# Scores of a batch's last two attention tasks in four quarters of the array, and another order of pools, in a fused attention and mixture-of-experts kernel

## The chip, the cores and the metric

One core of a Trainium2 chip runs one program. The metric is the device time of one execution in microseconds, as the median over runs. The kernel before takes 660.11 us (three runs, 658.83 to 661.78).

## What is computed

```python
def _attn_ref(q, k, v):                      # B, H, S, D = 8, 8, 576, 64
    scores = np.matmul(q, k.transpose(0, 1, 3, 2)) / np.sqrt(D)
    rel = pos[:, None] - pos[None, :]
    mask_local = (rel >= 0) & (rel < 32)
    mask_strided = (rel >= 0) & (pos[None, :] % 32 == pos[:, None] % 32)
    # heads 0 to 3 use mask_local, heads 4 to 7 mask_strided; softmax; times v

def _moe_ref(x, w_gate, w1, w2):             # N, D, E, F = 4608, 512, 8, 1024
    probs = softmax(x @ w_gate); expert = argmax(x @ w_gate)
    # row by row: probs[expert] * (relu(x @ w1[expert]) @ w2[expert])
```

The rows of x are the 4608 tokens with the outputs of their 8 heads side by side.

## The kernel before

**Attention.** Only the score blocks that a mask leaves are computed. The blocks of one batch are laid out in five tasks k = 0 to 4 (`BANK_PAIRS`), each of which fills one PSUM bank `s` of 128x512 f32. Tasks 0 and 1 are local heads, task 2 holds a rest of the local heads and three strided blocks, tasks 3 and 4 hold strided blocks alone, of 54x54 and, four in task 3, of 36x36. There are 40 tasks, and one loop goes over them in slots. In the slot of task i, the program emits in this order: the transposition of the probabilities of task i-3 (`stage_t`, L460, bank `t`), small steps from a queue (logits L535 and L542, rows of x L527, routing L577, L625), the scores of task i (`stage_s`), the load of q and k for task i+5 (`load_qk`, issued on SP), the product with v of task i-4 (`av_local` L485 or `av_strided` L474, banks `v`), and the load of v for a later task (`load_v`, SP). From batch 4 on, every slot also carries pieces of early expert windows (`filling`), which need expert weights (`raw`, L214, SP) that ACT casts to `whi` (L222) and DVE to `wlo` (L223).

TensorE runs in the order in which the program emits; the other engines and SP are ordered by a scheduler that estimates when each instruction can start. There are two banks `s`. Tasks take them in turn.

`stage_s` first adds the mask to the whole bank with one 128x512 matmul (L408), then adds the blocks. A strided block of the pair's head h reads partitions 64h to 64h+63 and writes the same partitions of the bank (L430): h = 0 uses one quarter of the array, h = 1 the quarter diagonally opposite. Then `softmax` follows on a bank: maximum `nm` (L357, DVE), subtraction into the tile `prob` (L360, DVE, the last reader of the bank), exponential (L361, ACT), sum `sm` (L363) and reciprocal `ri` (L365, L366, DVE), product `prob` (L367, POOL). ACT copies results out of PSUM (L162): `pT`, `xT`, `xr`.

**Experts.** `window` gathers 256 or 512 tokens of one expert by an indirect DMA on POOL (L240), splits them in two f32r parts, multiplies by w1 (L302 to L304, `t`), splits the result (`hh` L307 on ACT, `hl` L308 on DVE), multiplies by w2 (L291 to L293), scales (`finish`, L258 on ACT or L260 on DVE) and scatters the rows by an indirect DMA on POOL (L261). The main loop over `ORDER` starts with expert 1. Tiles of 32 tokens (`small`) have their weights loaded by ACT's queue (`sraw`, L1027, behind a register load from `srow`, L1005). The pools behind attention (`yp` for the output rows, `slp` for slots, `smp` for small tiles) are placed in SBUF that attention's pools have given back, in the order in which they are made. Who uses such a place first waits for its last user of before.

Of the kernel before, what the change touches and what calls it, by code (L numbers as in the profile page):

```python
# [1 line left out]

# [22 lines left out]
RG = 3 * SR  # L25
NRG = 11
LASTG = S - (NRG - 1) * RG
# [39 lines left out]
NBK = len(BANK_PAIRS)  # L67
WHERE = {p: (k, n) for k, ps_ in enumerate(BANK_PAIRS) for n, p in enumerate(ps_)}
LB = 16


def task_layout():
# [71 lines left out]
def moe_attn(ctx, tc, qk, vv, wg, wcat, blob0, blob, out):  # L144
    nc = tc.nc
# [7 lines left out]
    def bank(tag):  # L153
        return ps.tile([128, 512], F32, name=tag, bufs=BANKS[tag])
# [170 lines left out]
    with ExitStack() as actx:  # L325
# [76 lines left out]
            o = VV[k][0][key] + 128 * n  # L402
            return loaded[b, "v", k][:, o:o + 128]

        def stage_s(b, k):
            sb = bank("s")
            mk = 0 if k < 2 else k - 1 if k < 3 else 2
            nc.tensor.matmul(sb, identb, mask_b[:, mk].rearrange("p n k -> p (n k)"), start=True, stop=False)  # L408

            t = loaded.get((b, "qk", k))  # L410
            at = QK[k][0]

            def wide(m, i, last):
                j = 4 * m + i
                keys = qkl[k][:, LQ:].rearrange("p (h x) -> p h x", h=2)[:, :, QB * j:QB * j + 64]
                o = sb[QB * i:QB * i + QB, 256 * (m // 2):256 * (m // 2) + 256].rearrange("p (h y c) -> p h y c", h=2, y=2)
                nc.tensor.matmul(o[:, :, m % 2], qkl[k][:, QB * j:QB * j + QB], keys,  # L417
                                 start=False, stop=last, tile_position=(0, QB * i))

            def local(o0, nb, i, h, j, col, last):  # L420
                hs = slice(64 * h, 64 * h + 64)
                o = 64 * h + 32 * i
                q0 = o0 + QB * j
                k0 = q0 + QB * nb
                nc.tensor.matmul(sb[o:o + QB, col:col + 64], t[hs, q0:q0 + QB], t[hs, k0:k0 + 64],
                                 start=False, stop=last, tile_position=(64 * h, o))

            def strided(q0, k0, w, h, col, last):
                hs = slice(64 * h, 64 * h + 64)
                nc.tensor.matmul(sb[64 * h:64 * h + w, col:col + w], t[hs, q0:q0 + w], t[hs, k0:k0 + w],  # L430
                                 start=False, stop=last, tile_position=(64 * h, 64 * h))

            for n, (kind, hp, m) in enumerate(BANK_PAIRS[k]):
                if kind == "l":
                    for i in range(4):
                        wide(m, i, m == 3)
                    continue
                for y in range(2):
                    col = 128 * n + 64 * y
                    last = n == 3 and y == 1  # L440
                    if kind == "lx":
                        for i in range(2):
                            for h in range(2):
                                local(at["lx", i], 2, i, h, y, col, last)
                    else:
                        for h in range(2):
                            if kind == "s":
                                q0 = at["s", hp, m] + RG * y
                                strided(q0, q0 + 2 * RG, RG, h, col, last)
                            else:  # L450
                                q0 = at["sx", y]
                                strided(q0, q0 + LASTG, LASTG, h, col, last)
            return softmax(sb)

        pTs = {}

# [9 lines left out]
            evac("a", pT, tb)  # L466
            pTs[b, k] = pT

        def probs_of(b, pair, y, cols):
            k, n = WHERE[pair]  # L470
            return pTs[b, k][64 * y:64 * y + 64, 128 * n + cols.start:128 * n + cols.stop]

        def av_mm(av, c0, w, h, y, lhsT, rhs):
            nc.tensor.matmul(av[64 * h:64 * h + 64, c0:c0 + w], lhsT, rhs, start=True, stop=True, tile_position=(64 * y, 64 * h))  # L474
# [14 lines left out]
        def av_strided(b, hp, xT, off):  # L489
            av = [bank("v"), bank("v")]  # L490
            for t in range(5):
                vst = v_of(b, WHERE["s", hp, t][0], ("s", hp, t))
                for y in range(2):
                    for h in range(2):
                        av_mm(av[y], RG * t, RG, h, y, vst[64 * y:64 * y + RG, 64 * h:64 * h + 64],
                              probs_of(b, ("s", hp, t), y, slice(64 * h, 64 * h + RG))[0:RG])
            c1 = 5 * RG
            if hp == 0:
                for i in range(2):
                    vt = v_of(b, 2, ("lx", i))  # L500
                    for y in range(2):
                        for h in range(2):
                            av_mm(av[y], c1 + QB * i, QB, h, y, vt[64 * y:64 * y + 64, 64 * h:64 * h + 64],
                                  probs_of(b, ("lx", 0, 4), y, slice(64 * h + 32 * i, 64 * h + 32 * i + 32)))
            else:
                vst = v_of(b, 3, "sx")
                for y in range(2):
                    for h in range(2):
                        av_mm(av[y], c1, LASTG, h, y, vst[64 * y:64 * y + LASTG, 64 * h:64 * h + 64],
                              probs_of(b, ("sx", 0, 5), y, slice(64 * h, 64 * h + LASTG))[0:LASTG])  # L510
            xv = xT[:, 2 + hp, off:off + S].rearrange("p (a r) -> p r a", r=STR)
            for y in range(2):
                dst = xv[:, 0:30, :].rearrange("p (t y l) a -> p t y l a", y=2, l=3)[:, :, y, :, :]
                evac("a", dst, av[y][:, 0:c1].rearrange("p (t l a) -> p t l a", l=3, a=SR))
                if hp == 0:
                    x0 = off + 512 + QB * y
                    evac("a", xT[:, 0:2, x0:x0 + QB], av[y][:, c1:c1 + 2 * QB].rearrange("p (a q) -> p a q", q=QB))
                else:
                    xl = xT[:, 2 + y, off:off + S].rearrange("p (a r) -> p r a", r=STR)
                    evac("a", xl[:, 30:32, :], av[y][:, c1:c1 + LASTG].rearrange("p (r a) -> p r a", a=SR))  # L520
# [322 lines left out]
        tasks = [(b, k) for b in range(B) for k in range(NBK)]  # L843
# [25 lines left out]
        pvs = {}  # L869
        with tc.manual_schedule(engines={mybir.EngineType.PE}):  # L870
            for i in range(nt + LAG_AV):
# [4 lines left out]
                ia = i - LAG_AV  # L876
# [8 lines left out]
                    step()  # L885
                if i < nt:
                    filling()
                    pvs[i] = stage_s(*tasks[i])
                    load_qk(i + NBK)
                if 0 <= ia < nt:  # L890
                    if k == 0:
                        queue.extend(late)
                        late.clear()
# [43 lines left out]
    pools.append((wraw2, whl2))  # L937
    xgm = ctx.enter_context(tc.tile_pool(name="xgm", bufs=8))
    xtm = ctx.enter_context(tc.tile_pool(name="xtm", bufs=2))
    yp = ctx.enter_context(tc.tile_pool(name="yp", bufs=5))  # L940
    slp = ctx.enter_context(tc.tile_pool(name="slp", bufs=2))
    smp = ctx.enter_context(tc.tile_pool(name="smp", bufs=1))

    def slot(sid, so, load):
        xg = gather(xgm, sid)
# [125 lines left out]
    side = []  # L1071
# [22 lines left out]
    for i in range(len(jobs)):  # L1094
# [12 lines left out]
                issue_after(drained[0], lastp[0])  # L1107
        if ORDER[i][0] == "w":
            drain_(side.pop())
        elif i == 1:  # L1110
            next(smalls[0])
        cur = nxt

# [118 lines left out]
```

## Time and profile before

| | |
|---|---|
| median of the runs | 660.11 us |
| the profiled execution, its own time | 667.39 us |
| its span, first to last instruction | 665.60 us |
| TensorE busy, share of the span | 613.0 us, 92% |
| mean granted TensorE clock | 0.97 |
| attention | until about 200 us of the span |

The profile comes from one execution. Its pages give, for each engine, the busy time, groups of instructions by source line, what ended an idle stretch, and timelines. A matmul in f32 shows as two records. PE is TensorE, PEld its weight loads, DVE VectorE, ACT ScalarE, POOL GpSimd, SPq the DMA queue of SyncE, ACTq that of ScalarE.

### The profile page before, as it was taken

The numbers are of one execution on the slowest core, as the hardware profiler recorded it, in microseconds if no ns is written. First come the engines' busy times: TensorE is split into PE (matmuls) and PEld (weight loads), VectorE is DVE, ScalarE is ACT, GpSimd is POOL, SyncE is SP. The second block draws the span as 40 slices with busy tenths as digits, with TensorE's granted clock in tenths as the row PEclk, the third lists the DMA queues.
The fourth block names the chain that finished last, engine by engine and source line by source line (L and its number), as shares of the span: only waits on it lengthen the run. The fifth ranks groups of instructions, "written<-read, shape, count | busy, mean of one in ns | idle before, by whom it ended". The sixth has DMA issues, their size and how long they took to land.

```text
span 665.6 us, 14957 instructions
## 1 busy us (share of the span) xinstructions
PE 613.0 (92%) x6136; PEld 508.5 (76%) x6154; DVE 402.0 (60%) x773; ACT 324.7 (49%) x568; POOL 149.5 (22%) x168
## 2 busy tenths in 40 slices
PE   4889888789888989999899799999999999999996
PEld 3667757568767778987688698787888788887885
DVE  5758959757763569988433576723776225863332
ACT  1646757645546355355332555523655224753232
POOL 4323322332211021224101313201512004301021
PEclk9989989989979889999999999999999999999999
DMA  9969999995548274658934686763886546964301
GB/s 283 261 207 297 308 307 306 334 331 191 203 143 269 77 279 144 238 165 314 378 113 137 229 290 228 271 230 127 308 311 226 182 163 238 356 205 154 120 20 64
DMA packets 36549, 149.85 MB, mean 225 GB/s; under 512 B 5114, under 2 KB 5504, under 8 KB 26240
## 3 DMA queue, kind: packets, MB, share of 16 engines
q1 hardware_dynamic: 22848, 105.92, 48.1%
q10 hardware_dynamic: 7344, 22.70, 9.6%
q0 software_dynamic: 6288, 20.26, 8.2%
q8 instruction: 49, 0.80, 0.5%
q14 instruction: 20, 0.16, 0.1%
HBM read 129.69 MB, written 19.63 MB: 224 GB/s over the span
## 4 chain that ended last, share of the span: by engine, by line
issue 43%; PE 31%; DMA 9%; POOL 7%; DVE 6%; ACT 2%; another core or an unknown queue 1%; POOLq 1%; SPq 0%; ACTq 0%; DVEq 0%
POOL xg L240 4%; POOL out_dram L261 3%; DMA xd<-xr 3%; PE t L302 3%; PE t L303 3%; PE t L304 3%; PE y L291 2%; PE y L293 2%; PE y L292 2%; PE s L417 2%; PE s L430 2%; PE t L460 2%; DMA qkl<-in_qk_dram 2%; PE v L485 2%; DMA out_dram<-y,oids 2%
## 5 line engine op out<-in xcount | busy, mean ns | idle before, releaser
L223 DVE TENSOR_TENSOR wlo<-raw,whi 128x1024 fp32r<-128x1024 f32 x136 | 164.8, 1232 | 78.3 <-ACT whi L222 73.2
L222 ACT CAST whi<-raw 128x1024 fp32r<-128x1024 f32 x136 | 139.2, 1051 | 62.8 <-PE s L293 25.5
L302 PE MATMUL t<-xh,whi 128*128 128x256 f32 (+1 forms) x384 | 126.6, 331 | 1.6 <-ACT xh L231 1.5
L303 PE MATMUL t<-xl,whi 128*128 128x256 f32 (+1 forms) x384 | 124.0, 323 | 0.9 <-DVE xl L232 0.5
L304 PE MATMUL t<-xh,wlo 128*128 128x256 f32 (+1 forms) x384 | 122.9, 321 | 0.0
L308 DVE SCALAR_TENSOR_TENSOR hl<-t,hh 128x256 fp32r<-128x256 f32 (+1 forms) x96 | 48.8, 509 | 98.8 <-ACT hh L307 98.6
L307 ACT ACTIVATE hh<-t 128x256 fp32r<-128x256 f32 (+1 forms) x96 | 43.7, 455 | 120.4 <-PE t L304 118.1
L302 PEld LDWEIGHTS t<-xh,whi 128*128 128x128 f32 x384 | 73.2, 191 | 13.5 <-issue 4.4
L291 PE MATMUL y<-whi,hh 128*128 128x512 f32 x192 | 77.2, 402 | 2.7 <-ACT hh L307 2.7
L303 PEld LDWEIGHTS t<-xl,whi 128*128 128x128 f32 x384 | 73.7, 192 | 7.6 <-DVE xl L232 1.0
L304 PEld LDWEIGHTS t<-xh,wlo 128*128 128x128 f32 x384 | 73.5, 192 | 5.3
L292 PE MATMUL y<-wlo,hh 128*128 128x512 f32 x192 | 75.9, 395 | 0.0
L293 PE MATMUL y<-whi,hl 128*128 128x512 f32 x192 | 75.1, 396 | 0.1
L367 POOL TENSOR_TENSOR prob<-prob,ri 128x512 f32<-128x512 f32 x40 | 43.4, 1084 | 114.5 <-DVE ri L366 86.4
L261 POOL DMA_INDIRECT out_dram<-y,oids x24 | 26.5, 1104 | 123.7 <-DVE y L260 118.8
L291 PEld LDWEIGHTS y<-whi,hh 128*128 128x128 f32 x192 | 36.4, 190 | 9.5 <-ACT hh L307 3.8
L162 ACT COPY xT<-v 128x270 f32<-128x270 f32 (+1 forms) x80 | 30.8, 473 | 25.5 <-PE v L474 10.9
L293 PEld LDWEIGHTS y<-whi,hl 128*128 128x128 f32 x192 | 35.9, 189 | 9.1 <-DVE hl L308 1.2
L292 PEld LDWEIGHTS y<-wlo,hh 128*128 128x128 f32 x192 | 36.5, 190 | 4.9
L361 ACT ACTIVATE prob<-prob 128x512 f32<-128x512 f32 x40 | 25.4, 635 | 28.5 <-DVE prob L360 28.2
L363 DVE TENSOR_REDUCE sm<-prob 128x8 f32<-128x512 f32 x40 | 27.3, 683 | 18.6 <-ACT prob L361 17.8
L357 DVE TENSOR_REDUCE nm<-s 128x8 f32<-128x512 f32 x40 | 27.3, 683 | 15.1 <-PE s L430 8.4
(219 smaller groups left out, 1030.7 us busy)
## 6 DMA issues: line engine op xcount, KB each, us to landing
raw<-in_wcat_dram SPq DMA_DIRECT2D x68, 1024.0 KB
sraw<-in_wcat_dram ACTq DMA_DIRECT2D x12, 1024.0 KB
xd<-xr ACTq DMA_DIRECT2D x36, 264.0 KB
vl<-in_vv_dram SPq DMA_DIRECT2D x16, 512.0 KB
qkl<-in_qk_dram SPq DMA_DIRECT2D x16, 264.0 KB
vt<-in_vv_dram SPq DMA_DIRECT2D x16, 256.0 KB
qk<-in_qk_dram SPq DMA_DIRECT2D x8, 484.0 KB
qk<-in_qk_dram SPq DMA_DIRECT2D x8, 432.0 KB
```

The source lines that it names most:

```text
L222: nc.scalar.copy(out=hi[:, sl], in_=raw[:, sl])
L223: i = nc.vector.tensor_tensor(out=lo[:, sl], in0=raw[:, sl], in1=hi[:, sl].bitcast(F32), op=ALU.subtract)
L261: i = nc.gpsimd.indirect_dma_start(out=out, out_offset=bass.IndirectOffsetOnAxis(ap=idc, axis=0), in_=y, in_offset=None, bounds_check=N - ...
L291: nc.tensor.matmul(yb[t], hh[:, ts], whi[:, w], start=(j == 0), stop=False)
L292: nc.tensor.matmul(yb[t], hh[:, ts], wlo[:, w], start=False, stop=False)
L293: nc.tensor.matmul(yb[t], hl[:, ts], whi[:, w], start=False, stop=(j == 7))
L302: nc.tensor.matmul(hb[:, 0:n], whi[:, w], xh[:, dc, :], start=(dc == 0), stop=False)
L303: nc.tensor.matmul(hb[:, 0:n], whi[:, w], xl[:, dc, :], start=False, stop=False)
L304: nc.tensor.matmul(hb[:, 0:n], wlo[:, w], xh[:, dc, :], start=False, stop=(dc == 3))
L307: nc.scalar.activation(out=hh[:, 0:n], in_=hb[:, 0:n], func=AF.Relu)
L308: nc.vector.scalar_tensor_tensor(out=hl[:, 0:n], in0=hb[:, 0:n], scalar=0.0, in1=hh[:, 0:n].bitcast(F32), op0=ALU.max, op1=ALU.subtract)
L367: product[0] = nc.gpsimd.tensor_tensor(out=pv, in0=pv, in1=ri.unsqueeze(2).broadcast_to([128, 8, 64]), op=ALU.mult)
```

## The change

The scores of tasks 3 and 4 of a batch are made together in the slot of task 3, into both banks `s`. Task 4 has its heads swapped in the bank (`side`): head 0 writes partitions 64 to 127 and head 1 partitions 0 to 63, so that it uses the two quarters of the array that task 3 leaves free. The generators `scores` of the two tasks take turns after every two blocks. The slot of task 4 makes no scores. The product with v reads the swapped columns. Behind attention the pool `yp` is made after `slp` and `smp`, and the first step of the first small tile is emitted after the first job of the main loop and not after the second.

```diff
+PAIR = (3, 4)
+        def side(k, h):
+            return 1 - h if k == PAIR[1] else h
...
-        def stage_s(b, k):
-            sb = bank("s")
+        def scores(b, k, sb):
             mk = 0 if k < 2 else k - 1 if k < 3 else 2
             nc.tensor.matmul(sb, identb, mask_b[:, mk].rearrange("p n k -> p (n k)"), start=True, stop=False)
...
+            yield
...
-                nc.tensor.matmul(sb[64 * h:64 * h + w, col:col + w], t[hs, q0:q0 + w], t[hs, k0:k0 + w],
-                                 start=False, stop=last, tile_position=(64 * h, 64 * h))
+                o = 64 * side(k, h)
+                nc.tensor.matmul(sb[o:o + w, col:col + w], t[hs, q0:q0 + w], t[hs, k0:k0 + w],
+                                 start=False, stop=last, tile_position=(64 * h, o))
...
-            return softmax(sb)
+                    yield
+
+        def stage_s(b, *ks):
+            sb = [bank("s") for _ in ks]
+            gens = [scores(b, k, s) for k, s in zip(ks, sb)]
+            for _ in zip_longest(*gens):
+                pass
+            return [softmax(s) for s in sb]
...
-                    pvs[i] = stage_s(*tasks[i])
+                    b, k = tasks[i]
+                    if k == PAIR[0]:
+                        pvs[i], pvs[i + 1] = stage_s(b, *PAIR)
+                    elif k not in PAIR:
+                        pvs[i], = stage_s(b, k)
...
-    yp = ctx.enter_context(tc.tile_pool(name="yp", bufs=5))
     slp = ctx.enter_context(tc.tile_pool(name="slp", bufs=2))
     smp = ctx.enter_context(tc.tile_pool(name="smp", bufs=1))
+    yp = ctx.enter_context(tc.tile_pool(name="yp", bufs=5))
...
-        elif i == 1:
+        elif i == 0:
             next(smalls[0])
```

How the instructions stand on TensorE in batch 1, from task 3 on, before (`identb` and `mask_b` are the mask's operands):

```order
L408 LDWEIGHTS identb
L408 MATMUL s<-mask_b,identb 128x512
L430 MATMUL s<-qk 54x54 x8
L430 MATMUL s<-qk 36x36 x4
L430 MATMUL s<-qk 54x54 x4
L474 MATMUL v<-pT,vt 64x54 x20
L474 MATMUL v<-pT,vt 64x36 x4
L460 MATMUL t<-cst_70,prob 128x128 x4
L408 LDWEIGHTS identb
L408 MATMUL s<-mask_b,identb 128x512
L430 MATMUL s<-qk 54x54 x16
L535 MATMUL y<-xT,wg_sb 32x384 x4
```

and with the change (L413 is the mask, L437 a strided block, L488 the product with v, L474 the transposition):

```order
L413 LDWEIGHTS identb
L413 MATMUL s<-mask_b,identb 128x512
L413 LDWEIGHTS identb
L413 MATMUL s<-mask_b,identb 128x512
L437 MATMUL s<-qk 54x54 x16
L437 MATMUL s<-qk 36x36 x2
L437 MATMUL s<-qk 54x54 x2
L437 MATMUL s<-qk 36x36 x2
L437 MATMUL s<-qk 54x54 x10
L488 MATMUL v<-pT,vt 64x54 x20
L488 MATMUL v<-pT,vt 64x36 x4
L474 MATMUL t<-cst_70,prob 128x128 x4
```

Mask and blocks of task 4 have moved ahead of the product with v and of the next transposition, right behind and between those of task 3.

ACT's order at the start of batch 6, before (`whi<-raw` is the cast of expert weights; two casts belong to one load):

```order
L162 COPY pT<-t 128x512
L222 CAST whi<-raw 128x1024
L552 ACTIVATE ex<-dl 128x24
L162 COPY xT<-v 128x512 x2
L361 ACTIVATE prob<-prob 128x512
L162 COPY xr<-v 128x512
L162 COPY pT<-t 128x512
L530 DMA xd<-xr 128x528
L162 COPY xr<-v 128x512
L222 CAST whi<-raw 128x1024
L530 DMA xd<-xr 128x528
```

and with the change:

```order
L164 COPY pT<-t 128x512
L224 CAST whi<-raw 128x1024 x2
L566 ACTIVATE ex<-dl 128x24
L164 COPY xT<-v 128x512 x2
L164 COPY xr<-v 128x512
L363 ACTIVATE prob<-prob 128x512
L544 DMA xd<-xr 128x528
L164 COPY pT<-t 128x512
L164 COPY xr<-v 128x512 x2
```

The first of the casts of before (the second half of the first load) has moved into batch 5. Both halves of the second load now stand where it stood, ahead of the copies `xT` and `xr`. On SP, that second load has moved ahead of the last four loads of q, k and v of its batch, and the third load ahead of ten.

ACT's first load of a small tile's weights, behind the start of expert 1, with what each instruction waits for, before:

```order
L1005 TENSOR_LOAD srow [waits DVE_49]
L1027 ISA
L1027 DMA sraw<-in_wcat_dram 128x2048 [waits DMASW4_49,DMASW3_49,DMASW5_49,DMASW1_49,DMASW7_49,DVE_49,Activation_49]
L307 ACTIVATE hh<-t 128x512 [waits PE_49]
L231 CAST sxh<-v 128x512 [waits PE_49]
```

and with the change:

```order
L1024 TENSOR_LOAD srow [waits DVE_49]
L1046 ISA
L1046 DMA sraw<-in_wcat_dram 128x2048 [waits DMASW5_49,DMASW1_49,DMASW7_49,DVE_49,Activation_49]
L309 ACTIVATE hh<-t 128x512 [waits PE_49]
L233 CAST sxh<-v 128x512 [waits PE_49]
```

The load stands in the same place. Its waits for DMASW4 and DMASW3 are gone: in the program these two counts are reached by the last two scatters of the window before (L261, the rows of expert 0), and the other DMASW counts by gathers and a scatter much earlier. The output tiles `y` of the main loop wait for them instead.

## Rows read from the trace of the kernel before

**Rows 1.** The page: busy time of TensorE and its weight loads, share, instructions.
```profile
PE 613.0 (92%) x6136; PEld 508.5 (76%) x6154; DVE 402.0 (60%) x773; ACT 324.7 (49%) x568; POOL 149.5 (22%) x168
```
**Rows 2.** Windows: busy us by engine, granted clock, DMA share, GB/s.
```profile
100.00:120.00 20.00, 17.23 (x403) 13.58 (x395) 19.30 (x59) 14.67 (x31) 5.78 (x11) 1.00 1.01 310
120.00:140.00 20.00, 14.62 (x298) 12.03 (x297) 13.52 (x29) 12.44 (x23) 7.87 (x10) 0.83 0.97 312
```
**Rows 3.** Timeline of PE, batch 2: start, us, instruction, records [idle before, releaser].
```profile
50.38 0.96 PE L474 MATMUL v<-pT,vt 54*64 54x54 f32 x54
51.27 0.66 PE L460 MATMUL t<-cst,prob 128*128 128x128 f32 x4
51.76 0.38 PE L408 MATMUL s<-mask_b,identb 128*128 128x512 bf16 x1
52.07 0.90 PE L430 MATMUL s<-qk 64*54 64x54 f32 x29
...
52.87 1.31 PE L474 MATMUL v<-pT,vt 54*64 54x54 f32 x47
...
54.91 1.01 PE L430 MATMUL s<-qk 64*54 64x54 f32 x32
55.85 1.70 PE L535 MATMUL y<-xT,wg_sb 128*32 128x384 f32 x16
```
**Rows 4.** Timelines: DVE's subtraction of task 2, PE's mask of task 3.
```profile
30.13 0.68 DVE L360 TENSOR_TENSOR prob<-s,nm 128x512 f32<-128x512 f32 x1
51.79 0.68 DVE L360 TENSOR_TENSOR prob<-s,nm 128x512 f32<-128x512 f32 x1
112.06 0.68 DVE L360 TENSOR_TENSOR prob<-s,nm 128x512 f32<-128x512 f32 x1
29.65 0.38 PE L408 MATMUL s<-mask_b,identb 128*128 128x512 bf16 x1
111.42 0.38 PE L408 MATMUL s<-mask_b,identb 128*128 128x512 bf16 x1
```
**Rows 5.** Timelines of PE and POOL: what follows the scores of task 4.
```profile
20.82 0.66 PE L460 MATMUL t<-cst,prob 128*128 128x128 f32 x4 [0.42 <-POOL prob L367]
73.64 1.04 POOL L367 TENSOR_TENSOR prob<-prob,ri 128x512 f32<-128x512 f32 x1 [1.27 <-PE t L460]
41.30 0.55 PE L542 MATMUL y<-cst,ls 128*128 128x128 f32 x3 [0.74 <-DVE ls L158]
98.35 0.55 PE L542 MATMUL y<-cst,ls 128*128 128x128 f32 x3
```
**Rows 6.** Timelines of SP, ACT and PE around the start of batch 6.
```profile
113.86 0.37 SPq L392 DMA_DIRECT2D qk<-in_qk_dram  x1
118.10 0.48 SPq L214 DMA_DIRECT2D raw<-in_wcat_dram  x1
122.61 0.59 ACT L162 COPY xT<-v 128x512 f32<-128x512 f32 x1 [1.15 <-PE v L485]
129.92 1.05 ACT L222 CAST whi<-raw 128x1024 fp32r<-128x1024 f32 x1 [1.92 <-DMA raw<-in_wcat_dram]
123.43 0.66 PE L527 MATMUL v<-cst,xT 128*128 128x128 f32 x4
132.02 1.71 PE L474 MATMUL v<-pT,vt 54*64 54x54 f32 x52 [3.39 <-ACT xr L162]
135.31 0.47 PE L280 MATMUL v<-cst,xg 128*128 128x128 f32 x1 [1.58 <-ACT xT L162]
```
**Rows 7.** Timelines of POOL, ACT and PE at the start of expert 1.
```profile
318.91 0.99 POOL L261 DMA_INDIRECT out_dram<-y,oids  x1 [0.30 <-issue]
325.55 0.36 ACTq L1027 DMA_DIRECT2D sraw<-in_wcat_dram  x1
325.95 0.60 ACT L307 ACTIVATE hh<-t 128x512 fp32r<-128x512 f32 x1 [4.64 <-PE t L304]
326.60 0.50 PE L291 MATMUL y<-whi,hh 128*128 128x512 f32 x1 [1.15 <-ACT hh L307]
```

More of the change, by code (lines that the diff above doesn't have):

```diff
@@ L1 @@
 from contextlib import ExitStack
+from itertools import zip_longest
 import concourse.bass as bass
@@ L467, in stage_t, with probs_of @@
             pTs[b, k] = pT
-        def probs_of(b, pair, y, cols):
+        def probs_of(b, pair, y, c, w):
             k, n = WHERE[pair]
-            return pTs[b, k][64 * y:64 * y + 64, 128 * n + cols.start:128 * n + cols.stop]
+            return pTs[b, k][64 * y:64 * y + 64, 128 * n + c:128 * n + c + w]
         def av_mm(av, c0, w, h, y, lhsT, rhs):
@@ L495, in av_strided @@
                         av_mm(av[y], RG * t, RG, h, y, vst[64 * y:64 * y + RG, 64 * h:64 * h + 64],
-                              probs_of(b, ("s", hp, t), y, slice(64 * h, 64 * h + RG))[0:RG])
+                              probs_of(b, ("s", hp, t), y, 64 * side(WHERE["s", hp, t][0], h), RG)[0:RG])
             c1 = 5 * RG
@@ L503, in av_strided @@
                             av_mm(av[y], c1 + QB * i, QB, h, y, vt[64 * y:64 * y + 64, 64 * h:64 * h + 64],
-                                  probs_of(b, ("lx", 0, 4), y, slice(64 * h + 32 * i, 64 * h + 32 * i + 32)))
+                                  probs_of(b, ("lx", 0, 4), y, 64 * h + 32 * i, 32))
             else:
@@ L509, in av_strided @@
                         av_mm(av[y], c1, LASTG, h, y, vst[64 * y:64 * y + LASTG, 64 * h:64 * h + 64],
-                              probs_of(b, ("sx", 0, 5), y, slice(64 * h, 64 * h + LASTG))[0:LASTG])
+                              probs_of(b, ("sx", 0, 5), y, 64 * h, LASTG)[0:LASTG])
             xv = xT[:, 2 + hp, off:off + S].rearrange("p (a r) -> p r a", r=STR)
@@ L887, in moe_attn @@
                     filling()
-                    pvs[i] = stage_s(*tasks[i])
+                    b, k = tasks[i]
[3 more added lines that the diff above has]
+                        pvs[i], = stage_s(b, k)
                     load_qk(i + NBK)
                 if 0 <= ia < nt:
+                    b, k = tasks[ia]
                     if k == 0:
```

## The prediction

> **What bounds the kernel now.** I read the busy table first. TensorE works 613.0 of 665.6 us [rows 1]: an instruction that leaves its path, or runs faster on it, shortens the kernel unless something else is late at that place. Then windows of 20 us over attention. The reader sees there that TensorE is not alone: from 100 to 120 us DVE is busy 19.30 of 20 us and the DMA engines' share is 1.01; from 120 to 140 us the DMA share is 0.97, TensorE works 14.62 us and its granted clock is 0.83 [rows 2]. So a gain on TensorE early in attention can be kept, while around batches 4 to 6 it may turn into waiting. Third, TensorE's timeline through one batch [rows 3], which gives the pace of each kind of matmul; last, timelines of DVE, POOL, ACT and SP at each place where the change moves something. The sum is made against the profiled execution, 667.39 us, 7.28 us or 1.1% above the median of 660.11; I carry differences over to the median.
>
> **1. The pair's scores.** Task 4's 32 records start at 54.91 and the next instruction at 55.85: 0.94 us. Task 3's 32 records (29 of them seen) run from 52.07 to 52.87: 0.80 us [rows 3]. Together 1.74 us for 64 records, 27.2 ns each. They use two quarters of the array, both into one bank. The product with v uses all four quarters and two banks: 54 records from 50.38 to 51.27, 16.5 ns each [rows 3]. The pair has the same shape of work, so I take that pace: 64 x 16.5 = 1.06 us, 0.68 less per batch, 8 x 0.68 = **-5.4**. One bound is the present pace, a gain of 0. The other is half the present pace, 13.6 ns, as if two more quarters were free of cost: 0.87 x 8 = -7.0. A loss I exclude at this term: today too, two quarters with different rows write one bank, and each bank gets no more writers than now. The masks stay two steps of 52.07 - 51.76 = 0.31 us [rows 3].
>
> Here a page speaks against the change. The Trainium skill, "TensorEngine Tiling (Array Packing)", section Restrictions and Gotchas, says that different row tiles cannot access the same PSUM bank at the same time. Each bank of the pair is still written by two row tiles, so by that rule the quarters would take turns as today and this term be 0; by the row it is -5.4. No run so far shows two banks of scores at once; it is rival D.
>
> **2. The second mask's wait.** The pair needs both banks at once, and the second is that of task 2, whose last reader is DVE's subtraction. What queues behind the waiting mask is everything on TensorE: the pair's scores, the product with v, the next transposition. First mask done against subtraction done [rows 3, 4]:
> - batch 1: 29.65 + 0.31 = 29.96 against 30.13 + 0.68 = 30.81, a wait of 0.85
> - batch 2: 52.07 against 51.79 + 0.68 = 52.47, a wait of 0.40
> - batch 5: 111.42 + 0.31 = 111.73 against 112.06 + 0.68 = 112.74, a wait of 1.01
>
> In the five other batches the subtraction ends before the first mask does. Sum **+2.26**. If each of the five came late by the mean of the three, 0.75, it would be +6.0; if DVE, with task 4's softmax moved, were ahead at all three, 0.
>
> **3. The next transposition.** Task 4's scores stand today between the pair's first half and the transposition of task 2, and cover that task's way through DVE, ACT and POOL. In batch 0 the transposition already waits 0.42 for POOL's product; in batch 3 the product ends only at 73.64 + 1.04 = 74.68, and a transposition that comes earlier waits for it [rows 5]. In these two the saving is lost: 2 x 0.68 = **+1.36** (bounds 0 and 8 x 0.68 = +5.4).
>
> **4. Task 4's old slot.** In batch 4 its scores stand between two groups of logits, and the second of these, at 98.35, waits for nothing. In batch 1 the same group waits 0.74 for DVE's `ls` [rows 5]. Without the cover batch 4 may wait so too, at most by what it saved: **+0.68** (bounds 0 and 0.68).
>
> **5. Casts in batch 6.** ACT now runs a cast ahead of the copies `xT` and `xr` that TensorE waits for. TensorE waits there 3.39 us for `xr` and 1.58 for `xT`, 4.97 in all; the load `raw` was issued at 118.10 and its cast began at 129.92 after a wait of 1.92: 11.8 us from issue to cast [rows 6]. With the change the load moves ahead of four loads, to about 113.86 [rows 6]; with the same 11.8 us the cast starts at 125.7. Two casts of 1.05, then `xT` at 0.59, end at 128.4; the matmul that now starts at 123.43 would wait 128.4 - 123.43 = 5.0 us. Then `xr`, no longer behind a cast, is in time, and the two waits of today go. 5.0 against 4.97: **0**. Where the raw weights are there when ACT comes, the cast needs no wait: ACT is free today at 122.61 - 1.15 = 121.46, and 1.05 earlier, at 120.4, without the cast that moves into batch 5. Two casts and the copy end at 120.4 + 2.1 + 0.59 = 123.1, and with the second copy of `xT`, 0.59, and the short exponentials at some 124.2: a wait of up to 0.8, and the term is 0.8 - 4.97 = -4.2. Where they land no earlier than today, 129.92 + 2.1 + 0.59 = 132.6, a wait of 9.2, +4.2; as the gathers and copies behind it are late as well I give the upper end +6. On SP the loads of q, k and v that are passed are used some 20 us later and more: nothing.
>
> **6. Behind attention.** At the start of expert 1 ACT waits 4.64 us, its next instruction `hh` runs at 325.95, and TensorE then waits 1.15 for it [rows 7]. ACT's load `sraw`, issued at 325.55, stood between: it waits for the last scatters, one of them issued on POOL at 318.91 [rows 7]. The change takes those two waits from `sraw` and gives them to the tiles `y`, which are written so much later (one window is some 18 us of matmuls) that the scatters have landed: 0 there. So the 1.15 go: **-1.15** (bounds 0, if `hh` itself was late, and -1.15). The first small tile's earlier step moves no row on TensorE and costs 0.
>
> **Sum:** -5.4 + 2.26 + 1.36 + 0.68 + 0 - 1.15 = -2.25. 667.39 - 2.25 = 665.1 for a profile like this one, and 660.11 - 2.25 = **657.9** on the median, 0.34% less. About 0.5%, 3.3 us, is what a measurement of this kernel can tell from no change: the bounds are 656.8 and 663.4.
>
> **Rivals.**
> - **A, more is kept.** The raw weights are there in time (step 5 gives -4.2), and task 4's earlier softmax puts DVE ahead in batch 1, so that its 0.85 goes. 657.9 - 4.2 - 0.85 = 652.8. For it: the load is issued earlier by 4.2 us and the cast waited only 1.92 [rows 6]. Against it: DMA share of 1.01 and 0.97 [rows 2]; a load moved ahead in a full queue gains, but its own 11.8 us need not shrink.
> - **B, absorbed.** DVE at 19.30 of 20 us and the DMA engines at 1.01 [rows 2] set the pace of attention, and every saving of step 1 comes back as a wait at a mask, a transposition or a cast. What remains is step 6: 660.11 - 1.15 = 659.0. Against it: batches 0 to 3 hold waits of under 1 us for other engines [rows 5].
> - **C, slower.** One mechanism: ACT's in-order queue at the start of batch 6. The cast blocks ACT until the raw weights land, no earlier than today (129.92), and `xT`, the exponentials and `xr` stand behind it: +4.2 to +4.4 in step 5, 660.11 - 2.25 + 4.4 = 662.3. TensorE's idle stretch grows with it, and the clock was already 0.83 from 120 to 140 us: a fall to 0.83 over 20 us is 20 x 0.17 x 2 = 6.8 us at the lower level of 1.2 GHz instead of 2.4 GHz, in which 3.4 us of work are lost. One more such stretch gives 662.3 + 3.4 = 665.7. It decides against the forecast from a landing later than about 128 us. For it: the full DMA engines. Against it: the load is issued 4.2 us earlier.
> - **D, it doesn't do what it says.** The scores' pace stays 27.2 ns as two halves with different rows still write one bank: 657.9 + 5.4 = 663.3. Against it: 27.2 ns is reached today by just such halves. For it: the product with v, my only row at 16.5 ns, also has two banks, but none of its rows tells which two quarters share one. The rule of the Trainium skill's section named in step 1 would give this time.
>
> **How the numbers follow.** Forecast 0.40 (own range 655 to 660.5, of it 0.10 below 656.8), A 0.30, B 0.10, C 0.15 (0.02 of it below 663.4), D 0.05 (0.02 of it below 663.4). Faster by over 0.5%: 0.30 + 0.10 = 0.40. Within: 0.30 + 0.10 + 0.02 + 0.02 = 0.44. Slower: 0.13 + 0.03 = 0.16. The range goes from 651.5, rival A with 1.3 more of step 1's far bound (-7.0 + 5.4 = -1.6), to 663.5, which takes in D and half of C's way. What is left out is most of C, 0.13, and some 0.06 of A. Cases of both signs hold most of the chance, so the forecast's own range stands above.
>
> **What would show it.** Step 1: the pair's 64 blocks take about 1.06 us and not 1.74. Step 2: in batches 1, 2 and 5 the second mask has a wait for DVE of 0.4 to 1.0. Step 3: the transposition of task 2 waits for POOL in batches 0 and 3. Step 5: ACT's cast behind the start of batch 6 waits for `raw`, TensorE waits some 5 us before the product that writes `xr`'s bank, and none later; a cast without a wait is A, one that ends past 130 us is C. Step 6: ACT issues `sraw` early, and the 1.15 before the first product with w2 of expert 1 is gone. The prediction is wrong if the granted clock falls in a stretch where it was 1.00, if masks wait in all eight batches, or if a load passed on SP comes late.

## The result and the profile after

| | before | with the change |
|---|---|---|
| median, of three runs and of four | 660.11 us | 653.16 us |
| ratio, 95% interval | | 0.9887 (0.9843 to 0.9932) |
| the profiled execution: its time, its span | 667.39, 665.60 us | 652.89, 651.0 us |
| mean granted clock of that execution | 0.97 | 0.99 |

The medians, and the means further down, leave out the few runs that fell into a slower state, here one of before with 668.90 us, and the first profiled execution of before is such a run too. The kernel is 1.1% faster where 0.3% was forecast. Two later comparisons, on two chips, gave 0.9929 (0.9898 to 0.9960) and 0.9897 (0.9851 to 0.9944), so some 5 to 7 us.

The page of the profile after, TensorE's totals and its row of the granted clock (one digit for each fortieth of the span):

```profile
PE 599.2 (92%) x6139; PEld 495.9 (76%) x6154; DVE 402.2 (62%) x773; ACT 325.1 (50%) x568; POOL 148.9 (23%) x168
PEclk9799999899999999999999999999999999999999
```

Windows of the kernel after, columns as in [rows 2]:

```profile
100.00:120.00 20.00, 14.26 (x369) 11.43 (x365) 18.68 (x53) 14.04 (x30) 5.09 (x9) 0.98 0.98 317
120.00:140.00 20.00, 17.42 (x389) 13.87 (x390) 14.72 (x34) 13.44 (x28) 7.99 (x10) 0.93 0.93 308
```

Against [rows 2], 2.97 us less work from 100 to 120 us, the same full DVE and DMA engines, and a clock of 0.93 instead of 0.83 behind it (0.83 also in a second profile of before). TensorE's busy time fell by 13.8 us, more than the scores could give, because matmuls at half clock are busy longer: task 4's 32 records in the first trace of before took 1.74 us in batch 1, at half clock, and 1.01 in batch 2. In the two traces the stretches at a granted clock of 0.5 add up to 37.3 us before and 15.0 after. The first profiled execution of before lost more to them than a second one, which has 26.0, so 14.6 us of span is not the size of the change, and the tables below use means over runs.

TensorE in batch 5, kernel after, start, us, instruction, records [idle before, releaser]:

```profile
110.78 0.38 PE L413 MATMUL s<-mask_b,identb 128*128 128x512 bf16 x1
112.66 0.39 PE L413 MATMUL s<-mask_b,identb 128*128 128x512 bf16 x1 [1.50 <-DVE prob L362]
112.97 0.97 PE L437 MATMUL s<-qk 64*54 64x54 f32 x62
113.77 0.22 PE L488 MATMUL v<-pT,vt 54*64 54x54 f32 x1
118.48 0.85 PE L549 MATMUL v<-xT,wg_sb 128*32 128x384 f32 x6 [2.88 <-ACT xT L164]
```

The second mask waits 1.50 for DVE's subtraction, as step 2 said, where [rows 4] gave 1.01. The pair then takes 113.77 - 112.97 = 0.80 us, not 1.06. Behind it stands a wait that was not in the prediction: the first logits of the third group wait 2.88 us for ACT's copy `xT`.

From the table of TensorE's waits in the first 205 us, kernel after (engine, line, releaser: us in all, times, longest), without the 5.0 us at the start that both kernels have:

```profile
PE t L474 <- POOL prob L369: 4.2, 2, 2.6
PE v L549 <- ACT xT L164: 3.1, 2, 2.9
PE y L556 <- DVE ls L160: 2.7, 4, 0.8
PE v L488 <- issue: 2.6, 1, 2.6
PE s L437 <- issue: 2.5, 4, 1.0
PE s L413 <- DVE prob L362: 2.3, 3, 1.5
```

and of a second profile of the kernel before, taken with the experiments:

```profile
PE v L280 <- ACT xT L162: 3.1, 2, 2.3
PE t L460 <- POOL prob L367: 2.7, 2, 2.6
PE y L542 <- DVE ls L158: 2.5, 3, 1.2
PE v L474 <- ACT xr L162: 2.2, 1, 2.2
PE v L474 <- DVE xl L232: 2.0, 1, 2.0
```

Of the waits of the second list, at the starts of batches 6 and 7, that of the product with v for `xr` is gone, that for `xl` fell to 0.6, and that of L280 for `xT` (now L282) to 1.7. What is new are the masks, the logits' wait for `xT`, and pauses inside the pair's blocks put down to "issue", in which TensorE waits for nothing that the profile shows.

### The profile page after: what moved, and what is told of

Same layout as the page of the kernel before. It is cut to its first block, busy times and chain, and to the rows that moved or that the text cites. A ratio compares the mean times of both kernels' runs of the same rounds, so it can differ in the third digit from the quotient of the medians.

```text
span 651.0 us, 14957 instructions
## 1 busy us (share of the span) xinstructions
PE 599.2 (92%) x6139; PEld 495.9 (76%) x6154; DVE 402.2 (62%) x773; ACT 325.1 (50%) x568; POOL 148.9 (23%) x168
## 4 chain that ended last, share of the span: by engine, by line
issue 33%; PE 28%; POOL 6%; DMA 3%; DVE 2%; ACT 2%; POOLq 1%; another core or an unknown queue 0%; ACTq 0%; DVEq 0%
PE t L306 4%; PE t L305 4%; PE t L304 4%; PE y L295 3%; POOL xg L242 3%; PE y L293 3%; PE y L294 3%; POOL out_dram L263 2%; DMA xd<-xr 1%; ACT whi L224 1%; DMA raw<-in_wcat_dram 1%; DVE wlo L225 1%; PE v L541 1%; PE v L282 1%; PE s L295 1%
## 5 line engine op out<-in xcount | busy, mean ns | idle before, releaser
L304 PEld LDWEIGHTS t<-xh,whi 128*128 128x128 f32 x384 | 72.1, 189 | 12.8 <-issue 3.0
L242 POOL DMA_INDIRECT xg<-xd,ids x24 | 28.3, 1181 | 31.6 <-DVE y L262 22.1
L365 DVE TENSOR_REDUCE sm<-prob 128x8 f32<-128x512 f32 x40 | 26.7, 680 | 13.5 <-ACT prob L363 13.4
```

What stands on the lines that cost most here:

```text
L242: lastp[0] = nc.gpsimd.indirect_dma_start(out=xg, out_offset=None, in_=xd[0:rows, :], in_offset=bass.IndirectOffsetOnAxis(ap=idc, axis=0))
L304: nc.tensor.matmul(hb[:, 0:n], whi[:, w], xh[:, dc, :], start=(dc == 0), stop=False)
```

## Experiments

Two theories went into them. **W**: the gain is work and waits that left TensorE's path. **C**: most of it is the clock: the pair takes away idle stretches behind which TensorE falls to the lower of its two levels. To tell them apart the runs of each series are split: a stretch at half clock loses half its length, so span x (1 - mean clock) is counted as lost to the lower level, and the rest of the span as work and waits at full clock. It is an upper bound: it counts TensorE's idle time within such a stretch, and stretches in which another engine sets the pace. The table has means, with the medians of the same runs; the runs of one series share a chip.

| series, kernel | runs | median us | clock | lost to the clock, us | rest of the span, us |
|---|---|---|---|---|---|
| 1, before | 19 | 661.4 | 0.9805 | 12.8 | 646.2 |
| 1, the same again | 10 | 662.1 | 0.9806 | 12.8 | 647.6 |
| 1, pools only | 11 | 659.6 | 0.9795 | 13.5 | 644.3 |
| 1, pair only | 6 | 655.5 | 0.9857 | 9.4 | 644.4 |
| 1, pair in two quarters | 6 | 652.9 | 0.9890 | 7.2 | 644.7 |
| 2, before | 29 | 653.6 | 0.9815 | 12.1 | 639.9 |
| 2, before, waits filled | 8 | 649.9 | 0.9866 | 8.7 | 639.2 |
| 2, after | 12 | 649.8 | 0.9838 | 10.5 | 636.6 |
| 2, later second mask | 12 | 653.2 | 0.9827 | 11.3 | 640.0 |
| 2, after, start filled | 12 | 651.2 | 0.9820 | 11.7 | 637.7 |
| 3, before | 15 | 654.6 | 0.9796 | 13.3 | 639.0 |
| 3, after | 6 | 648.7 | 0.9842 | 10.2 | 636.7 |
| 3, pair in two quarters | 5 | 647.3 | 0.9892 | 7.0 | 638.3 |
| 3, pair only | 12 | 652.3 | 0.9828 | 11.2 | 637.7 |
| 3, after, two waits filled | 6 | 647.3 | 0.9867 | 8.6 | 637.7 |

The standard errors are 0.4 to 1.5 us for the clock's part and 0.3 to 1.0 for the rest. The two rows of the unchanged kernel in series 1 differ by 1.4 in the rest, so a single difference below that says nothing.

**The kernel before, again.** No edit.

> The kernel before, unchanged, for a second profile. Theory W (the gain of the change is work and waits taken off TensorE's path): 660.5 us, ratio 1.000, and the same long waits as in the first profile, among them the 3.4 us at the start of batch 6 and the 2.0 us in batch 7. Theory C (most of the gain is that fewer stretches run at the lower clock): the same time, and again some six to eight stretches at the granted clock of 0.5, 25 to 37 us in all, against 15 us of the changed kernel, so that 5 to 11 us of the difference are the clock's.

0.9996 to 1.0067 around a ratio of 1.0032. Its trace has 26.0 us at half clock, of it 6.8 us from 130 and 3.4 us from 185 us, behind the same two waits as in the first trace. Both theories keep these waits; that the falls come back at the same places is what C needs.

**Pools only.**

```diff
-    yp = ...            (ahead of slp, smp)
+    yp = ...            (behind slp, smp)
-        elif i == 1:
+        elif i == 0:
             next(smalls[0])
```

> The kernel before with the new order of pools and the earlier first small tile, without the pair of scores. My step 6 (only the 1.15 us ahead of expert 1's first product with w2 goes): 660.9 - 1.15 = 659.8 us, ratio 0.998. Rival (the pools carry more: the two profiles, less half of their stretches at the lower clock, stand 0.7 us apart at the end of the early windows and -2.8 at the end, so 3.5 us come from behind attention): 657.4 us, ratio 0.995, with about 1.3 of it between 430 and 490 us.

659.55 us, ratio 0.9966 (0.9934 to 0.9998): faster by 0.3%, in the table all of it in the rest of the span. The place is that of step 6. TensorE ahead of its first product with w2 of expert 1, pair without the new pools, and ACT there:

```profile
315.28 0.50 PE L293 MATMUL y<-whi,hh 128*128 128x512 f32 x1 [1.99 <-ACT hh L309]
314.23 0.36 ACTq L1046 DMA_DIRECT2D sraw<-in_wcat_dram  x1
314.63 0.60 ACT L309 ACTIVATE hh<-t 128x512 fp32r<-128x512 f32 x1 [5.51 <-DMA out_dram<-y,oids]
```

Here the profile names the scatter itself. With the new pools `sraw` goes out early, and `hh` waits for its own matmuls alone (ACT, kernel after):

```profile
309.06 0.36 ACTq L1046 DMA_DIRECT2D sraw<-in_wcat_dram  x1
312.00 0.60 ACT L309 ACTIVATE hh<-t 128x512 fp32r<-128x512 f32 x1 [2.59 <-PE t L306]
```

The wait on TensorE was 1.15 in the first profile of before, 1.13 in the second and 1.99 here, 1.25 and 1.24 in two later traces with the old pools, and none in the nine traces with the new ones. The stretch around it, from and to the same TensorE instructions (those at 320 and 335 us in the first profile), takes 15.0 to 15.1 us in the four others and 15.8 here at full clock, and 13.5 to 13.6 in all nine with the new pools. So the mechanism is right, and the place gave 1.5 us where 1.15 was forecast. Of the rival's extra 1.3 us between 430 and 490 us the first trace of before has 1.4 above the shortest, and no other has more than 0.8.

**Pair only**, twice.

```diff
+    yp = ...            (ahead of slp, smp again)
-        elif i == 0:
+        elif i == 1:
             next(smalls[0])
```

> The changed kernel with the old order of pools and the first small tile where it was: the pair of scores alone. If the pair carries nearly all (step 6 at 1.15 us): 653.2 + 1.15 = 654.3 us, ratio 0.990. If the pools carry 3.5 us: 656.7 us, ratio 0.9935. In both the 1.15 us ahead of expert 1's first product with w2 are there again.

> The changed kernel with the old order of pools, for a second time, beside the changed kernel: what the pools give where the pair is there. If the load of the small tile's weights is what they free, with 1.15 us: 0.2% slower than the changed kernel. By the traces' stretch from the last early window to expert 1's end (55.9 us, against 53.3 of three kernels with the new order): 2 to 2.6 us, 0.3 to 0.4% slower.

First 655.51 us, ratio 0.9910 (0.9876 to 0.9944), then 652.25 us, 0.9958 (0.9921 to 0.9995). Both intervals take in the 0.9935 of the first expectation, and the first also its 0.990, so the runs do not decide between them. By the table the pair alone takes 1.8 and 1.3 us from the rest and 3.5 and 2.1 from the clock. Beside the changed kernel in series 3 it is 1.8 us longer in the mean span, with a standard error of 1.2, which agrees with the pools' 1.5.

The traces show the clock's part by place. Up to the same TensorE instruction, at 200 us in the first profile, three traces with the old scores take 195.6 to 200.6 us, and five of the pair in four quarters, with either order of pools, 187.0 to 193.4. Stretches at half clock lose 10.2 to 13.7 us of it in the three and 5.1 in each of the five. What is left, 185.3 to 186.9 against 181.9 to 188.2, is not told apart. (Variants of the changed kernel, further down, lose 8.5 to 10.2 there, so such stretches come and go with small shifts.)

**Pair in two quarters**, twice. All engines have the same order as in the changed kernel; only the quarters differ.

```diff
-            return 1 - h if k == PAIR[1] else h
+            return h
```

> The changed kernel with task 4's heads not swapped: the pair is made together, in the same order on every engine, but both tasks use the same two quarters. Theory W: the scores go back to 27 ns each, 0.68 us a batch, 5.4 in all: 658.5 us, ratio 0.9965. Theory O (the gain is the new order, which moves softmax, casts and copies and so shortens waits and idle stretches that lower the clock; the pace is hidden behind waits that shrink by as much): 653 to 655 us, ratio 0.988 to 0.991, while the pair's 64 records take 1.74 us each time.

> The pair without the swap of heads, for a second time, beside the changed kernel. In the traces its 64 blocks take 1.56 us a batch where they run without a pause, and 0.81 with four quarters: 0.75 us a batch, 6 us in all. If that were worth its time, it is 6 us or 0.9% slower than the changed kernel. If the four quarters run into pauses in which TensorE waits for nothing that the profile shows (2.5 to 6.2 us inside the pair's blocks, against 0.7 without the swap) and into the same masks and transpositions, it stands within 0.3% of the changed kernel (within 2 us), as the first call had it (652.9 and 653.2 us, on two chips).

652.90 us, ratio 0.9890 (0.9838 to 0.9942), then 647.32 us, 0.9848 (0.9796 to 0.9900). It is not slower than the changed kernel, whose mean in series 3 is 1.8 us higher (standard error 1.6): **the four quarters, the change's namesake, bring nothing that these runs can tell.** The work is saved all the same. TensorE in batch 5 of this kernel:

```profile
110.62 0.39 PE L413 MATMUL s<-mask_b,identb 128*128 128x512 bf16 x1 [1.50 <-DVE prob L362]
110.94 1.72 PE L437 MATMUL s<-qk 64*54 64x54 f32 x61
112.45 0.26 PE L488 MATMUL v<-pT,vt 54*64 54x54 f32 x1
116.44 2.57 PE L549 MATMUL v<-xT,wg_sb 128*32 128x384 f32 x8 [1.63 <-ACT xT L164]
```

The pair takes 112.45 - 110.94 = 1.51 us, against 0.80. But from the second mask to the first logits it is 116.44 - 110.62 = 5.82 us here and 118.48 - 112.66 = 5.82 us in the changed kernel: the 0.71 saved, and some 0.5 by which the product with v behind the pair took longer here, became a longer wait for `xT`, 2.88 instead of 1.63. In series 3 the rest is 1.6 us longer than that of the changed kernel and 3.2 us less are lost to the clock, with standard errors of 1.2 and 1.7. Over both series the clock's part is 7.1 us in 11 runs here and 10.4 in 18 of the changed kernel. That TensorE, with more work, idles less and so keeps its clock would explain it; no run shows that link.

**Before, with two waits filled.** The added matmuls write a bank that the products fill next; the order of every engine is otherwise that of before.

```diff
             av = [bank("v"), bank("v")]
+            for _ in range({(5, 0): 8, (6, 1): 6}.get((b, hp), 0)):
+                nc.tensor.matmul(av[0], identb, mask_b[:, 0]..., start=True, stop=True)
```

> The kernel before with 14 more matmuls on TensorE, whose results are written over and never read: 8 of 128x512 bf16 (0.31 us each, 2.5 us) ahead of the product with v of batch 5's first pair, 6 (1.9 us) ahead of that of batch 6's second, both into the bank that this product fills anyway. In three profiles of the kernel before and of the pools alone, TensorE waits there 2.2 to 3.6 us each time (0.5 in one) for its second bank, and right behind, at 130 to 142 us and 184 to 193 us, the granted clock falls to 0.5 for 3.4 to 6.8 us; the profiles of the kernels with the pair have neither. Theory C (idle stretches of TensorE bring the falls, and the pair gains by taking these two away): no falls, or shorter ones, at the two places, mean clock up by 0.003 to 0.008 and 656.5 to 659.5 us (ratio 0.992 to 0.997) although work is added. Theory W (the falls come with something else, the gain is work and waits): the falls stay and the time is 661.5 to 663 us, ratio 1.000 to 1.002.

649.86 us, ratio 0.9943 (0.9916 to 0.9970): **more work, and faster by 0.6%.** By the table 3.4 of the 4 us are the clock's, with a standard error of 0.9. In the same series the changed kernel has 649.84 us: filling two waits in the kernel before brought as much as the whole change. Windows of TensorE alone (busy, clock, DMA share, GB/s) in the second profile of before, then in this kernel:

```profile
120.00:140.00 20.00, 14.96 (x290) 0.83 0.97 305
180.00:200.00 20.00, 16.44 (x229) 0.91 0.46 153
```

```profile
120.00:140.00 20.00, 16.78 (x319) 0.86 1.00 322
180.00:200.00 20.00, 18.46 (x278) 1.00 0.52 173
```

In batch 7's start the fall is gone. In batch 6 it stayed: the fill covers the wait for `xr`, but 1.83 and 0.75 us for `xT` and a gather follow at once. TensorE of this kernel at both places:

```profile
129.47 1.90 PE L492 MATMUL v<-mask_b,identb 128*128 128x512 bf16 x7
134.15 0.39 PE L280 MATMUL v<-cst,xg 128*128 128x128 f32 x1 [1.83 <-ACT xT L162]
135.29 0.90 PE L280 MATMUL v<-cst,xg 128*128 128x128 f32 x3 [0.75 <-DMA xg<-xd,eids]
183.27 1.46 PE L492 MATMUL v<-mask_b,identb 128*128 128x512 bf16 x6
186.82 0.66 PE L280 MATMUL v<-cst,xg 128*128 128x128 f32 x4 [1.21 <-ACT xT L162]
```

Nothing but TensorE's idle time was touched, and the kernel got faster while the mean clock of its runs rose from 0.9815 to 0.9866: C's mechanism can carry microseconds. Which falls went, the trace does not tell. At batch 7 the 3.4 us at half clock are gone, but others stand at 90 and 213 us, and in sum it has 27.4 us against 26.0 of the second profile of before. The Trainium skill, page "TensorE: Matmul & The Clock Gate", section HAM oscillation, tells of a TensorE that waits for DMA between bursts, drops to the lower clock and starts the next burst there. At batch 7 the two traces agree: with the wait of 2.0 us for `xl` went the 3.4 us at half clock behind it.

**The changed kernel, again**, twice more. No edit.

> The changed kernel, unchanged, beside the kernel without the swap's twin of the last call (652.9 us, ratio 0.989). If the four quarters are worth their 0.68 us a batch on the path: 648 to 650 us, ratio 0.981 to 0.983. If that gain is taken back by waits at the next mask, transposition or product: 652.5 to 654 us, ratio 0.986 to 0.989. The mean clock tells the rest: 0.985 or higher, against 0.980 of the kernel before.

> The changed kernel once more, on one chip with the kernel without the swap and the kernel without the new pools, since the chips differ by 7 us in the same kernel. Two calls gave ratios of 0.989 and 0.993 against the kernel before. 0.988 to 0.993 again; the mean clock 0.003 to 0.005 above that of the kernel before, which is 2 to 3 us of its gain, and 3 us of the rest in work and waits.

649.84 us, ratio 0.9929 (0.9898 to 0.9960), and 648.73 us, 0.9897 (0.9851 to 0.9944). In the table the change takes 3.3 and 2.3 us from the rest and 1.6 and 3.1 from the clock. The times of the earlier expectation were set for another chip; by its ratios the first outcome, four quarters on the path (0.981 to 0.983), is out, and the mean clock of 0.9838 stayed below the 0.985 expected.

**A later second mask.**

```diff
+            for _ in range(5 if len(ks) > 1 else 0):
+                next(gens[0])
             for _ in zip_longest(*gens):
```

> The changed kernel with the second mask behind eight blocks of task 3 instead of right behind the first mask. It takes the wait for DVE's subtraction out of TensorE's way by about 0.22 us of work in each batch (8 blocks of 27 ns), so 0.22 to 0.6 us of the 2.3 us of waits, and gives up a quarter of the overlap, 0.17 us a batch, 1.4 us in all. If overlap is worth its time: +0.8 us, 654 us, ratio 0.988 to 0.990. If the overlap is worth nothing, since waits take it back: 652 to 653 us, ratio 0.986 to 0.988. ACT's order shifts at some places too, which is a cost or gain of its own that neither has a number for.

653.20 us, ratio 1.0002 (0.9979 to 1.0026): all of the gain is gone, which neither outcome had. The mask now stands behind ten blocks (eight, and two that the first turn adds), and that shift re-sorted DVE, ACT and SP. DVE and TensorE of this kernel in batch 4:

```profile
91.23 1.23 DVE L225 TENSOR_TENSOR wlo<-raw,whi 128x1024 fp32r<-128x1024 f32 x1 [3.56 <-ACT whi L224]
93.69 0.69 DVE L362 TENSOR_TENSOR prob<-s,nm 128x512 f32<-128x512 f32 x1
94.43 0.61 PE L413 MATMUL s<-mask_b,identb 128*128 128x512 bf16 x1 [2.93 <-DVE prob L362]
```

DVE stands 3.56 us in front of a weight step that waits for ACT's cast, the subtraction queues behind it, and the mask waits 2.93 us. In the changed kernel that subtraction runs at 87.91, ahead of its mask. The run tells nothing on the overlap. What it suggests is that the order of the other engines can be worth as much as the whole change; no run moves that order alone.

**The changed kernel with its start filled.**

```diff
             tb = bank("t")
+            for _ in range({(0, 0): 8, (0, 2): 4}.get((b, k), 0)):
+                nc.tensor.matmul(tb, identb, mask_b[:, 0]..., start=True, stop=True)
```

> The changed kernel with 12 more matmuls whose results are written over: 8 (2.5 us) ahead of the first transposition of probabilities, where TensorE waits 2.6 us for POOL, and 4 (1.2 us) ahead of the third, where it waits 1.1 to 1.6. In all profiles so far the granted clock falls to 0.5 for 3.4 to 6.8 us between 14 and 21 us. Theory C: no fall there, 1.7 to 3.4 us less, 650 to 651.5 us, ratio 0.983 to 0.986. Rival (the time there is set by DVE, POOL and the DMA engines, so that TensorE's pace is not on the path): 653 to 654 us, ratio 0.987 to 0.989, with or without the fall.

651.18 us, ratio 0.9959 (0.9926 to 0.9991), in the mean 2.3 us more than the changed kernel on that chip (standard error 1.0). The fall between 14 and 21 us is gone from its trace, but others stand at 36, 80 and 97 us, and the mean clock is 0.982 against 0.984. So C's outcome did not come: a fall taken away at one place was not time gained. As the mean clock did not rise, the run doesn't show what the fall at the start costs, and the rival's reason stays open.

**The changed kernel with two waits filled.**

```diff
+            for _ in range(5 if (b, k) == (5, 3) else 0):
+                nc.tensor.matmul(sb, identb, mask_b[:, mk]..., start=True, stop=True)
...
             lb = bank(XTAGS[g])
+            for _ in range(4 if (g, c3) == (2, 0) else 0):
+                nc.tensor.matmul(lb, identb, mask_b[:, 0]..., start=True, stop=True)
```

> The changed kernel with nine more matmuls whose results are written over: five (1.5 us) in front of task 3's mask in batch 5, and four (1.2 us) in front of the first logits of the third group, where TensorE then waits 1.5 us for the second mask and 1.6 to 2.9 us for ACT's copy. Behind these two waits every profile of the pair has a stretch at half clock, 117 to 128 us. Theory C: it goes, 1.7 us or 0.26% less than the changed kernel, if the first five, which stand ahead of the waiting mask and so delay task 3's scores, cost nothing. Rival (as at the start of the kernel: the stretch there is paced by DVE and the DMA engines): the same time as the changed kernel or up to 1.5 us more, with or without the fall.

647.25 us, ratio 0.9877 (0.9824 to 0.9930), beside 0.9897 of the changed kernel: not told apart. The fall at 117 to 128 us is not in its trace; in the table the clock gives back 1.6 us and the rest grows by 1.0, both within the noise. Two things blur it: the four added matmuls themselves wait 1.09 us for `xT`, whose copy frees the bank that they write, and DVE's order in batch 5 is another. Inconclusive.

## Why the prediction came out as it did

The sign and the range held (651.5 to 663.5); the forecast of 657.9 missed by 4.7 us, and the time came out at rival A's 652.8, of whose two reasons one held. That it meets A's number is luck: A's step 5 came to -1.6 and not -4.2, batch 1's wait stayed, at 0.38, and the clock, which A has no term for, made up the difference.

- **No term for the clock: the step that failed.** The sum was made at full clock. Its -2.25 answers to the rest of the span, which fell by 3.3 and 2.3 us in series 2 and 3; that they agree is in part luck, since steps 1 and 5 below miss in opposite directions. On top come 1.6 and 3.1 us of clock. The 0.83 of [rows 2] was read, but used only as a threat in rival C. The waits of [rows 6] that brought it were in the sum, priced at their idle time alone. And one of its signs of being wrong came: the granted clock fell where it had been 1.00, for 3.4 us from 119 us, behind the waits of batch 5.
- **Step 1, size right, effect wrong.** The pair runs at 0.80 to 0.81 us where it meets no pause, 12.7 ns a record: 0.93 us less than the 1.74 of before, beyond the far bound of 13.6 ns. Against the pair in two quarters, which itself takes 1.5, it is 0.7 a batch. The step took it as kept on the path. Beside the two-quarter runs none of it shows in the time. (The three records of task 3 that it did not see stand in the trace at 52.77, between records of the product with v.)
- **Step 2, right.** Forecast +2.26 in batches 1, 2 and 5; measured 2.3, as 0.38, 0.38 and 1.50.
- **Step 3, half right.** In batch 0 the wait for POOL grew from 0.42 to 1.58; in batch 3 none appeared. 1.16 against 1.36. Later traces of the changed kernel have 0.56 in batch 0 in one and 0.57 in batch 3 in another, so each is one sample.
- **Step 4, right**: a wait of 0.53 for `ls` in batch 4 (0.33 and 0.20 in two later traces), forecast at 0.68 at most.
- **Step 5, wrong.** It had one wait of 5.0 us replaced by another. The load of the raw weights went out at 110.89, not 113.86, and the casts began at 122.62 with no wait for it, 11.7 us later; the 4.97 us of [rows 6] shrank to 0.77, A's -4.2. But DVE now takes both maxima of the pair ahead of the first subtraction, ACT's exponential waits for that, and `xT` stands behind it on ACT: batch 5's logits wait 2.88 us where 0.31 was, +2.57. TensorE in the first trace of before, then SP, DVE, ACT and TensorE, kernel after:

```profile
117.31 1.37 PE L535 MATMUL v<-xT,wg_sb 128*32 128x384 f32 x8 [0.31 <-ACT xT L162]
```

```profile
110.89 0.42 SPq L216 DMA_DIRECT2D raw<-in_wcat_dram  x1
115.65 0.67 DVE L359 TENSOR_REDUCE nm<-s 128x8 f32<-128x512 f32 x1
116.32 0.68 DVE L359 TENSOR_REDUCE nm<-s 128x8 f32<-128x512 f32 x1
117.03 1.23 DVE L362 TENSOR_TENSOR prob<-s,nm 128x512 f32<-128x512 f32 x2
117.69 0.63 ACT L363 ACTIVATE prob<-prob 128x512 f32<-128x512 f32 x1 [1.65 <-DVE prob L362]
118.23 0.20 ACT L164 COPY xT<-v 128x36 f32<-128x36 f32 x1
122.62 2.00 ACT L224 CAST whi<-raw 128x1024 fp32r<-128x1024 f32 x2
133.95 0.66 PE L282 MATMUL v<-cst,xg 128*128 128x128 f32 x4 [0.77 <-ACT xT L164]
```

In another trace of the changed kernel that last wait is 1.94 us, followed by 1.27 for a gather, and there the granted clock falls to 0.5 for 3.4 us from 132 us; in this one it does not fall there.

- **Step 6, right mechanism, term slightly small**: 1.15 forecast, 1.5 in the traces.
- **Rivals.** B's absorption is what happened to step 1, in batch 5 to the last hundredth. C's landing past 128 us did not come. D is out: 12.7 ns a record. An estimate from [rows 3]: four f32 records of 128 columns on the whole array take 51.76 - 51.27 = 0.49 us, so one of 54 columns some 52 ns. The 27.2 ns of two quarters are half of that and the 12.7 ns of four a quarter, as if all quarters in use worked at once, although each bank takes results of two row tiles. By that estimate the rule of the Trainium skill, "TensorEngine Tiling (Array Packing)", section Restrictions and Gotchas, that different row tiles cannot access the same PSUM bank at the same time, does not hold for these tiles; that four quarters into two banks run at twice the pace of two would not speak against it alone.

What is not settled: how the clock's part divides between the waits that left batches 6 and 7 and idle time elsewhere. Filling two waits in the kernel before gave 3.4 us, so waits can carry it, while the two fills in the changed kernel gave nothing that the runs can tell; that the pair's gain is the same 1.6 to 3.5 us at the same places is argued from the traces, not shown by a run that gives them back to the changed kernel.

## What to carry over

Price a wait on TensorE at its idle time and, where the granted clock falls behind it in the trace, at half of that stretch too; a few useless matmuls in such a wait are a cheap test of it, though of the three such tests here only one made the kernel faster, and a fall taken away at one place can come back at another. Work taken off an engine counts only up to the next thing that is late: measure from the last common wait to the next one, as the 5.82 us here. Where a scheduler orders the other engines, look first at what a moved instruction does to their lists.

## What was not expected of the hardware

The pair's blocks hold a pause at a fixed place: in batch 1 TensorE stops after the 47th of the 64 records, in the changed kernel for 0.99, 3.69 and 0.32 us in three traces, and at the same record in two quarters, for 0.44 and 2.81. The longest of them, of a later trace of the changed kernel:

```profile
30.93 0.81 PE L437 MATMUL s<-qk 64*54 64x54 f32 x47
35.43 0.43 PE L437 MATMUL s<-qk 64*54 64x54 f32 x17 [3.69 <-issue]
```

No semaphore and no engine is named there, the DMA engines are nearly full around it, and the place goes with the program, which would suit instructions that arrive late; no run tried this. And one kernel, the one before, took 661, 654 and 655 us on three chips at the same mean clock of 0.98, so ratios are only taken within a series. Some 4.4 us of that stand at one place: between the same two TensorE instructions (those at 330 and 380 us in the first profile) six traces, those of before and after and all four of series 1, take 50.3 or 50.4 us, and all eight of series 2 and 3 take 45.9. In the six, TensorE, ACT and DVE all stand idle there, in a small tile; in the second profile of before ACT stands 2.50 us put down to "remote" and DVE 4.33 put down to "issue", neither of which names an engine. The cause is open.
